# An attention and MoE kernel on one core: its instruction order planned anew, with three small moves of work

## The chip, the cores and the metric

One core of a Trainium2 chip runs the kernel. The metric is the device time of one execution in microseconds (us); the time of a kernel is the median of several runs. One further execution is recorded by the hardware profiler, and all rows shown come from it. Engines: PE is TensorE (PEld its weight loads), DVE VectorE, ACT ScalarE, POOL GpSimd, SP SyncE, which issues nearly all transfers.

## The reference

Inputs are r, k, v, w of shape (4, 8, 768, 48), u (8, 48), and two weight matrices, 384 x 2048 and 2048 x 384. All is float32.

```python
for t in range(S):                                   # linear attention with decay w and bonus u
    cur = einsum('bhd,bhe->bhde', u * k[t], v[t])
    y[t] = einsum('bhd,bhde->bhe', r[t], state + cur)
    state = w[t][..., None] * state + einsum('bhd,bhe->bhde', k[t], v[t])
x = y as (3072 tokens, 384)
h = x @ w_in
g = where(h >= 1, h, where(h <= -1, 0, (h + 1) ** 2 / 4))
out = g @ w_out
```

## The kernel before, in words

The 3072 tokens are cut into 12 units of 256 tokens. `attention(u)` turns the recurrence of one unit into matmuls: VectorE scans the decays forward (L433) and backward (L428), scales k and r by them (L462, L512), TensorE multiplies within chunks of 64 tokens (L482), transposes k (L521, copied by ScalarE at L528), forms the chunks' updates of the state (L543) and sums the outputs (L592). Units 0 to 3 ("early") need k * u as well. In unit 0 ScalarE makes it (L453), in units 1 to 3 GpSimd (`with_u`, L444).

The result of a unit is x, kept as a high part rounded to the matmul type and a low part, the rest. ScalarE copies the high part out of PSUM (L649). The low part is made in one of two ways. For units in the set `INPLACE`, `less` has TensorE subtract the high part within PSUM by matmuls with minus the identity (L656, L658), and ScalarE copies what is left (L645). For all others VectorE subtracts (L647). One head pair's columns lie in a tile `last` and are spread into x by six small transfers on SyncE (x<-last, L691). Unit 0 does that by matmuls instead (`ALONE`).

Two units make a block of 512 tokens, six blocks in all. For each block and each of 16 slices f of the hidden layer, `products` has nine matmuls into h (L939), the gate on ScalarE and VectorE (L754, L755, L756, L758, L759), and nine matmuls into three accumulators `acc` (L959). Blocks 0 and 1 take their first 5 and 11 slices in halves of 256 tokens. The accumulators are copied out (L776) and sent off (L777).

`weight(f)` decodes slice f of the weights from raw 64-bit words: a transfer of 768 KB, two ScalarE passes (L354, L357), one GpSimd pass `rr` (L358), a VectorE pass (L360), then the split in high part (ScalarE, L350) and low part (VectorE, L363). At most `FLIGHT` = 3 raw slices are on their way.

No engine's order is written out by hand. Each operation is put into a `Plan` with its engine, an assumed cost in us, what it reads and writes, and a due time. `Plan.order` simulates the engines and picks, among the operations that are ready on an engine, the one with the earliest due time; `Plan.best` repeats this in six rounds with the steps' begin times of the round before, and keeps the shortest. The instructions are then issued in that order, each engine taking its own in turn. The due time of a unit's operation is the begin of the block's step that needs it, less `LEADS[u]` and `SLACK` times the rest of its chain; for weights it is `DECODES[f]`. `TURN` is the assumed cost of changing TensorE between 64-row and 128-row matmuls, `RATES` that of transfers. Where the plan sees TensorE idle, `kept_warm` fills in matmuls on zeros (L325).

At the end the kernel reads a flag (L825) and branches on it (L826) past a general fallback, which does not run for these inputs.

Of the kernel before, what the change touches and what calls it, by code (L numbers as in the profile page):

```python
# [48 lines left out]
class Plan:  # L49
# [9 lines left out]
    LATENCY = {"PE": 0.16, "DVE": 0.083, "ACT": 0.1}  # L59
    LATE_64 = 0.31  # L60

    TURN = {64: 0.22, 128: 0.09}
    RATES, SETTLED = (315e3, 400e3), 8.5
    ISSUE = 0.75

    def __init__(self):
# [63 lines left out]
    def order(self):  # L130
        ops = self.ops
        left = [len(op["deps"]) for op in ops]
        users = [[] for _ in ops]
        for n, op in enumerate(ops):
            for m in op["deps"]:
                users[m].append(n)
        free, end, begin, lands = {"SP": self.ISSUE}, {}, {}, []
        port = bus = 0.0
        mode = 128
        ran = {}  # L140
        open_ = {e: [] for e in ("PE", "SP", "ACT", "DVE", "POOL")}

        since = {}

        def opened(n):
            op = ops[n]
            since[n] = max((ran[m] if ops[m]["e"] == op["e"] and not ops[m]["size"] else end[m] + self.HOP for m in op["deps"]), default=0.0)
            open_[op["e"]].append(n)

        def ready(n):  # L150
            return max(since[n], port) if ops[n]["port"] else since[n]

        for n, k in enumerate(left):
            if not k:
                opened(n)
        first = {}
        while any(open_.values()):
            best = None
            for e, ns in open_.items():
                if not ns:  # L160
                    continue

                at = first.get(e)
                if at is None:
                    at = first[e] = min(ready(n) for n in ns)
                t = max(free.get(e, 0.0), at)
                if best is None or t < best[0]:
                    best = t, e
            t, e = best
            n = min((n for n in open_[e] if ready(n) <= t + 1e-9), key=lambda n: (ops[n]["key"], n))  # L170
            op = ops[n]
            open_[e].remove(n)
            first[e] = None
            if op["size"] and len(lands) >= LANES:
                t = max(t, lands[-LANES])
            begin[n] = t
            end[n] = t + op["cost"]
            if e == "PE" and op["mode"] != mode:
                mode = op["mode"]
                end[n] += self.TURN[mode]  # L180
            free[e] = ran[n] = end[n] - self.late(op)
            if op["port"]:
                port = free[e]
                first.clear()
            if op["size"]:
                bus = max(bus, t)
                bus += op["size"] / self.RATES[bus >= self.SETTLED]
                end[n] = bus + 2.0
                lands.append(end[n])
            for m in users[n]:  # L190
                left[m] -= 1
                if not left[m]:
                    opened(m)
                    first[ops[m]["e"]] = None
        assert len(begin) == len(ops)
        rank = sorted(range(len(ops)), key=lambda n: (begin[n], n))

        seen, out = set(), []

        def put(n):  # L200
            if n in seen:
                return
            seen.add(n)
            for m in sorted(ops[n]["deps"]):
                put(m)
            out.append(n)

        for n in rank:
            put(n)
        self.begin, self.end = begin, end  # L210
        return out

SLACK = 0.501
LEADS = {0: 89.12, 1: 29.14, 2: 50, 3: 29.29, 4: 70.5, 5: 42.42, 6: 96.05, 7: 79.29, 8: 141.79, 9: 131.35, 10: 73.56, 11: 100.77}
DECODES = [85.83, 12.47, 98.38, 2.07, 12.65, 0.37, -9.24, 7.4, -10.78, 23.04, -10.64, 54.35, 18.52, -29.87, 45.5, -17.01]
LEAD = 15
FLIGHT = 3

# [5 lines left out]


ALONE = {0}
INPLACE = {0, 6}
STEP, FIRST, PACED, AFTER = 17.0572, 293.658, 16.0129, 4.9  # L230
ROUNDS = 6


def attention_moe(tc, a):
    nc = tc.nc
# [101 lines left out]
    def weight(f, when):  # L337
        first, due = len(plan.ops), None
        s, k = fl[f % 2], f % 2
        m = s.bitcast(I32)  # L340
        r16 = rr.bitcast(U16).rearrange("p (c two) -> p c two", two=2)

        def fetch():
            wraw[f] = wpool.tile([128, 768, 2], I32, tag="wt", name=f"wraw{f}")
            nc.sync.dma_start(out=wraw[f].rearrange("p c two -> p (c two)"), in_=a["wbits"][f].bitcast(I32))

        def split():
            wt = wpool.tile([128, 2, 768], F32R, tag="wt", name=f"wt{f}")
            w_hi[f], w_lo[f] = wt[:, 0, :], wt[:, 1, :]
            A.copy(w_hi[f], s)  # L350

        op("SP", 0.45, due, (), [("raw", f), ("flight", f % FLIGHT)], fetch, size=786432)

        op("ACT", 0.9, due, [("raw", f)], [("fl", k)], lambda: A.activation(  # L354
            s, wraw[f][:, :, 1].bitcast(F32), AF.Abs, scale=float(2.0**-112)))
        op("ACT", 1.07, due, [("raw", f), ("flight", f % FLIGHT)], ["rr_low"],
           lambda: A.activation(r16[:, :, 0], wraw[f][:, :, 0].bitcast(U32), AF.Copy, scale=LOW))  # L357
        op("POOL", 3.2, due, [("raw", f)], ["rr_high"], lambda: G.tensor_scalar(  # L358
            out=r16[:, :, 1], in0=wraw[f][:, :, 1].bitcast(F32), scalar1=0.0, scalar2=32768.0, op0=ALU.is_lt, op1=ALU.mult))
        op("DVE", 0.95, due, ["rr_low", "rr_high"], [("fl", k)], lambda: V.scalar_tensor_tensor(  # L360
            out=m, in0=m, scalar=3, in1=rr, op0=ALU.logical_shift_left, op1=ALU.bitwise_or), port=True)
        op("ACT", 0.83, due, [("fl", k)], [("wh", f), ("raw", f)], split)
        op("DVE", 0.95, due, [("fl", k), ("wh", f)], [("wl", f)], lambda: V.tensor_tensor(  # L363
            out=w_lo[f], in0=s, in1=w_hi[f].bitcast(F32), op=ALU.subtract), port=True)
        plan.group(first, when, DECODES[f])

# [11 lines left out]
    def attention(u, when):  # L378
# [69 lines left out]
        for q in (1, 0):  # L448
            s = slot[q]
            if early:  # L450
                if alone:
                    for pr in range(2):
                        op("ACT", 0.42, due, [("k", s), "cst"], [("ku", q), "nk"], lambda q=q, pr=pr: A.activation(  # L453
                            ku[:, q, pr * UT : pr * UT + UT], rk[slot[q]][:, 1, pr * UT : pr * UT + UT], AF.Copy,
                            scale=u_col[:, 2 * q + pr : 2 * q + pr + 1]))
                else:
                    op("POOL", 2.85, due, [("k", s), "cst"], [("ku", q), "nk"], lambda q=q: with_u(q))
            op("DVE", 1.34, due, [("w", s)], [("p", q), "seeds"], lambda q=q: scan(q, False), port=True)
            op("ACT", 0.2, due, [("p", q)], [("ptot", u, q)], lambda q=q: A.copy(
                ptot[:, 4 * u + 2 * q : 4 * u + 2 * q + 2], pv[:, q, :, UT]))  # L460
            op("DVE", 1.48, due, [("w", s), ("p", q)], ["y", "seeds"], lambda q=q: scan(q, True), port=True)
            op("DVE", 0.69, due, ["y"], [("k", s)], lambda q=q: V.tensor_tensor(  # L462
                out=parts(q, 1), in0=parts(q, 1), in1=y_.rearrange("p (n c) -> p n c", c=UT + 1)[:, :, 1:], op=ALU.mult), port=True)
# [33 lines left out]
            for h in range(2):  # L497
                op("DVE", 0.73, due, [("b", bd[h]), "cst"], [("R", h)], lambda h=h: picked(h, bd[h], twice.bitcast(I32)))
        else:
            op("POOL", 1.9, due, (), ["nk"], lambda: G.tensor_tensor(  # L500
                out=nk[:, :, 0, :], in0=nk[:, :, 0, :], in1=nk[:, :, 1, :], op=ALU.mult), port=True)
            op("DVE", 0.94, due, ["us"], ["nk"], lambda: V.tensor_tensor(
                out=nk[:, :, 0, :], in0=nk[:, :, 0, :], in1=u_sb.unsqueeze(1).broadcast_to([128, 2, DM]), op=ALU.mult), port=True)
# [1 line left out]
                op("DVE", 0.54, due, ["nk"], ["d"], lambda c=c: V.tensor_reduce(  # L505
                    out=d_[:, c, :], in_=nk[:, c, 0, :].rearrange("p (h e) -> p h e", e=D), op=ALU.add, axis=AX.X))
            for h in range(2):
                op("POOL", 1.1, due, ["d", "cst"], [("R", h)], lambda h=h: G.tensor_tensor(  # L508
                    out=r_[h], in0=twice.unsqueeze(1).unsqueeze(1).broadcast_to([128, 4, 2, C]),
                    in1=dv[:, h].unsqueeze(3).broadcast_to([128, 4, 2, C]), op=ALU.mult), port=True)  # L510
        for q in (1, 0):
# [224 lines left out]
    def products(n):  # L736
# [8 lines left out]
        for half in range(2):  # L745
# [10 lines left out]
        op("DVE", 0.13 + 0.56 * k, due, [("b", 6 + hk)], [("g", gk)], lambda: nc.vector.scalar_tensor_tensor(  # L756
            out=gs, in0=gs, scalar=1.0, in1=hs, op0=ALU.min, op1=ALU.max))
        op("ACT", c, due, [("g", gk)], [("gh", gk)], lambda: nc.scalar.copy(ghs, gs))  # L758
        op("DVE", 0.15 + 0.54 * k, due, [("g", gk), ("gh", gk)], [("gl", gk)], lambda: nc.vector.tensor_tensor(  # L759
            out=gls, in0=gs, in1=ghs.bitcast(F32), op=ALU.subtract), port=True)  # L760
        count[b] = count.get(b, 0) + 1
        begin, end = count[b] == 1, f == NF - 1
# [16 lines left out]
        if done:  # L779

            out("DVE", nc.sync, "SP", 0, whole)
            out("ACT", nc.scalar, "ACT", 1, whole)
            out("DVE", nc.sync, "SP", 2, halves[0])
            out("ACT", nc.scalar, "ACT", 2, halves[1])
            return
        for j in range(3):
            out("ACT" if j else "DVE", nc.sync, "SP", j, whole)
# [241 lines left out]
```

## Time and profile before

| | |
|---|---|
| median of 3 runs | 525.49 us (525.31 to 525.93) |
| profiled execution | 525.05 us, span 523.0 us |
| granted TensorE clock, mean | 0.995 |
| busy: PE, DVE, ACT, POOL | 505.3, 333.5, 294.0, 108.2 us |
| matmuls | 5571 |
| transfers | 54.11 MB, mean 103 GB/s |
| last output's issue | 516.85 us |

The span is the time from the first to the last instruction of the profiled execution; the 2.05 us beside it lie outside. A row of a group gives line, engine, operation, tiles written <- read, count, busy time and mean duration, then the idle time of the engine before them and what ended it. "q" behind an engine (SPq, ACTq) is its queue of waits and transfers. A busy PE is not always useful: the fillers count too.

### The profile page before, as it was taken

The page shows a single profiled execution, that of the slowest core. Times are in us where ns is not written, and L with a number is a line of the kernel's source. Part 1 is how long each engine was busy: PE and PEld are TensorE (multiplying, and loading weights), DVE is VectorE, ACT ScalarE, POOL GpSimd, SP SyncE. Part 2 cuts the span into 40 slices and gives each one's busy share as a digit, 9 for nine tenths or more (in the row PEclk, how much of TensorE's full clock was granted, in tenths as well). Part 3 has the DMA queues.
Part 4 walks back from the last instruction along what each step waited for, and adds up shares of the span by engine and source line. Part 5 has one row for each costly group of instructions (what it writes and reads, how often), then busy time and mean ns, then how long its engine had stood idle before and what let it go on. Part 6 is the DMA issues. An engine that isn't in the chain of part 4 may idle for free.

```text
span 523.0 us, 13092 instructions
## 1 busy us (share of the span) xinstructions
PE 505.3 (97%) x5571; PEld 414.8 (79%) x5571; DVE 333.5 (64%) x561; ACT 294.0 (56%) x600; POOL 108.2 (21%) x72
## 2 busy tenths in 40 slices
PE   8899999999899999999999999999999999999994
PEld 7777977778899987877788788877777888888783
DVE  7899997749899996879872576242464333243331
ACT  3766798988765763765463456344354444444441
POOL 2896676602113111211110010000010000000000
PEclk9999999999999999999999999999999999999998
DMA  8965645136653512644400240000110000100001
GB/s 323 402 245 200 212 150 197 64 111 213 212 172 117 203 51 83 223 141 150 172 22 0 70 135 1 0 0 1 63 57 10 8 1 0 62 0 1 0 0 66
DMA packets 21921, 54.11 MB, mean 103 GB/s; under 512 B 3104, under 2 KB 8672, under 8 KB 21856
## 3 DMA queue, kind: packets, MB, share of 16 engines
q1 hardware_dynamic: 21568, 52.82, 29.4%
q8 instruction: 45, 0.74, 0.6%
q10 hardware_dynamic: 288, 0.39, 0.2%
q14 instruction: 20, 0.16, 0.1%
HBM read 46.32 MB, written 4.72 MB: 98 GB/s over the span
## 4 chain that ended last, share of the span: by engine, by line
PE 62%; DVE 14%; ACT 8%; DMA 7%; issue 4%; POOL 3%; SPq 2%; ACTq 0%; DVEq 0%; POOLq 0%
PE acc L959 28%; PE h L939 28%; PE bank L592 3%; POOL rr L358 3%; DMA rk<-in_rk 2%; DVE fl L360 2%; DMA wraw<-in_wbits 2%; DVE r L488 2%; DVE p L433 2%; DVE rk L512 1%; DMA x<-last 1%; DVE y L428 1%; PE bank L482 1%; DVE g L756 1%; DMA out_y<-g 1%
## 5 line engine op out<-in xcount | busy, mean ns | idle before, releaser
L939 PE MATMUL h<-x,wt 128*128 128x512 f32 (+1 forms) x1008 | 221.5, 367 | 2.9 <-DVE g L756 1.4
L939 PEld LDWEIGHTS h<-x,wt 128*128 128x128 f32 x1008 | 169.5, 188 | 37.9 <-DVE g L756 3.1
L959 PE MATMUL acc<-gh,wt 128*128 128x512 f32 (+1 forms) x672 | 155.9, 367 | 0.0
L756 DVE SCALAR_TENSOR_TENSOR g<-g,h 128x512 f32<-128x512 f32 (+1 forms) x112 | 67.8, 607 | 106.3 <-ACT g L755 105.4
L959 PEld LDWEIGHTS acc<-gh,wt 128*128 128x128 f32 x672 | 113.7, 188 | 22.2 <-ACT gh L758 0.9
L754 ACT ACTIVATE g<-h 128x512 f32<-128x512 f32 (+1 forms) x112 | 59.7, 533 | 93.2 <-PE h L939 85.9
L759 DVE TENSOR_TENSOR gl<-g,gh 128x512 fp32r<-128x512 f32 (+1 forms) x112 | 73.1, 655 | 36.6 <-ACT gh L758 35.8
L758 ACT CAST gh<-g 128x512 fp32r<-128x512 f32 (+1 forms) x112 | 62.3, 558 | 51.2 <-DVE g L756 49.1
L959 PE MATMUL acc<-gl,wt 128*128 128x512 f32 (+1 forms) x336 | 86.1, 364 | 0.0
L959 PEld LDWEIGHTS acc<-gl,wt 128*128 128x128 f32 x336 | 58.5, 188 | 11.6 <-DVE gl L759 0.8
L755 ACT ACTIVATE g<-g 128x512 f32<-128x512 f32 (+1 forms) x112 | 63.9, 571 | 3.3
L358 POOL TENSOR_SCALAR rr<-wraw 128x768 uint16<-128x768 f32 x16 | 55.1, 3441 | 31.7 <-DVE fl L360 17.2
L508 POOL TENSOR_TENSOR r<-cst,d 128x512 f32<-128x512 f32 x16 | 18.9, 1202 | 174.9 <-PE bank L592 134.5
L433 DVE TENSOR_TENSOR_SCAN p<-wq,seeds 128x514 f32<-128x514 f32 x24 | 31.5, 1313 | 3.1 <-POOL st L312 2.1
L428 DVE TENSOR_TENSOR_SCAN y<-wq,seeds 128x514 f32<-128x514 f32 x24 | 31.5, 1312 | 0.8
L500 POOL TENSOR_TENSOR nk<-nk 128x768 f32<-128x768 f32 x8 | 16.8, 2101 | 64.9 <-DMA nk<-in_nk 57.7
L528 ACT COPY kt<-bank 128x512 f32<-128x512 f32 x24 | 13.8, 583 | 17.8 <-PE bank L521 17.8
L357 ACT ACTIVATE rr<-wraw 128x768 uint16<-128x768 uint32 x16 | 17.4, 1089 | 4.6 <-DMA wraw<-in_wbits 2.5
L325 PE MATMUL bank<-clear 128*128 128x512 f32 (+1 forms) x60 | 17.6, 411 | 1.6 <-DVE seeds L432 1.6
L512 DVE TENSOR_TENSOR rk<-rk,p 128x512 f32<-128x512 f32 x24 | 17.9, 757 | 0.4 <-PE acc L482 0.4
L462 DVE TENSOR_TENSOR rk<-rk,y 128x512 f32<-128x512 f32 x24 | 17.7, 739 | 0.4 <-DMA rk<-in_rk 0.3
L592 PEld LDWEIGHTS bank<-rk,st 48*48 48x48 f32 (+1 forms) x656 | 11.5, 121 | 7.8 <-issue 2.2
(109 smaller groups left out, 393.4 us busy)
## 6 DMA issues: line engine op xcount, KB each, us to landing
rk<-in_rk SPq DMA_DIRECT2D x24, 512.0 KB, 5.1
wraw<-in_wbits SPq DMA_DIRECT2D x16, 768.0 KB, 6.9
wq<-in_w SPq DMA_DIRECT2D x24, 257.5 KB, 3.0
nk<-in_nk SPq DMA_DIRECT2D x8, 768.0 KB, 4.9
vn<-in_v SPq DMA_DIRECT2D x11, 384.0 KB, 6.4
fl<-in_w SPq DMA_DIRECT2D x12, 257.0 KB, 2.7
out_y<-g SPq DMA_DIRECT2D x10, 256.0 KB, 2.6
x<-last SPq DMA_DIRECT2D x66, 32.0 KB, 2.5
```

Source lines behind the costliest of these rows:

```text
L358: op("POOL", 3.2, due, [("raw", f)], ["rr_high"], lambda: G.tensor_scalar(out=r16[:, :, 1], in0=wraw[f][:, :, 1].bitcast(F32), scalar1=0.0 ...
L428: V.tensor_tensor_scan(out=y_[:, ::-1], data0=w[:, SEG:0:-1], data1=sv[:, ::-1], initial=0.0, op0=ALU.mult, op1=ALU.add)
L433: V.tensor_tensor_scan(out=pv[:, q].rearrange("p n c -> p (n c)"), data0=w[:, 0:SEG], data1=sv, initial=0.0, op0=ALU.mult, op1=ALU.add,)
L512: op("DVE", 0.69, due, [("p", q)], [("r", slot[q])], lambda q=q: V.tensor_tensor(out=parts(q, 0), in0=parts(q, 0), in1=pv[:, q, :, 0:UT], ...
L592: PE.matmul(out=bank[by[g]][HP * half : HP * half + wide, lo : lo + C], start=first, stop=False, skip_group_check=True, **kw)
L754: op("ACT", c, due, [("b", 6 + hk)], [("g", gk)], lambda: nc.scalar.activation(gs, hs, AF.Relu, scale=0.5, bias=0.5))
L755: op("ACT", c, due, (), [("g", gk)], lambda: nc.scalar.activation(gs, gs, AF.Square))
L756: op("DVE", 0.13 + 0.56 * k, due, [("b", 6 + hk)], [("g", gk)], lambda: nc.vector.scalar_tensor_tensor(out=gs, in0=gs, scalar=1.0, in1=hs, ...
L758: op("ACT", c, due, [("g", gk)], [("gh", gk)], lambda: nc.scalar.copy(ghs, gs))
L759: op("DVE", 0.15 + 0.54 * k, due, [("g", gk), ("gh", gk)], [("gl", gk)], lambda: nc.vector.tensor_tensor(out=gls, in0=gs, in1=ghs.bitcast( ...
L939: nc.tensor.matmul(hp, lhsT=wx[f][:, cs], rhs=xt[:, j, :], start=n == 0, stop=n == 8)
L959: nc.tensor.matmul(o[j], lhsT=wx[f][:, cs], rhs=gt, start=first and i == 0, stop=stop and i == 2, skip_group_check=True)
```

## The change

The planner's assumed costs and all its due-time parameters are new: turns, transfer rates and the landing of a transfer, GpSimd's passes, one VectorE cost, `SLACK`, `LEADS`, `DECODES`, `STEP`, `FIRST`, `PACED`. So every engine's order can differ. Three moves of work go with it: k * u of unit 1 is done by ScalarE (`SCALED`), as in unit 0; the low part of x of unit 1 is made in PSUM, and that of unit 6 no longer is (`INPLACE`); the last block's four outputs are all issued by SyncE, where ScalarE issued two.

```diff
-    TURN = {64: 0.22, 128: 0.09}
-    RATES, SETTLED = (315e3, 400e3), 8.5
+    TURN = {64: 0.33, 128: 0.02}
+    RATES, SETTLED = (315e3, 385e3), 8.5
...
-                end[n] = bus + 2.0
+                end[n] = max(bus + 2.0, t + 1.75 + op["size"] / 314e3)
...
-SLACK = 0.501
-LEADS = {0: 89.12, 1: 29.14, 2: 50, 3: 29.29, 4: 70.5, 5: 42.42, 6: 96.05, 7: 79.29, 8: 141.79, 9: 131.35, 10: 73.56, 11: 100.77}
-DECODES = [85.83, 12.47, 98.38, 2.07, 12.65, 0.37, -9.24, 7.4, -10.78, 23.04, -10.64, 54.35, 18.52, -29.87, 45.5, -17.01]
+SLACK = 1.384
+LEADS = {0: 200.34, 1: 17.94, 2: 10.1, 3: 21.34, 4: 40.45, 5: 51.11, 6: 84.54, 7: 119.23, 8: 114.23, 9: 96.67, 10: 78.32, 11: 100.22}
+DECODES = [58.08, 65.33, 175.35, 38.53, 1.42, 5.14, 81.19, 4.4, 14.07, 65.02, 61.72, 84.69, 39.36, 203.15, 25.09, -1.54]
...
-INPLACE = {0, 6}
-STEP, FIRST, PACED, AFTER = 17.0572, 293.658, 16.0129, 4.9
+INPLACE = {0, 1}
+SCALED = {0, 1}
+STEP, FIRST, PACED, AFTER = 27.1568, 703.402, 25.4941, 4.9
...
-        op("POOL", 3.2, due, [("raw", f)], ["rr_high"], ...
+        op("POOL", 3.35, due, [("raw", f)], ["rr_high"], ...
...
-                if alone:
+                if u in SCALED:
                     for pr in range(2):
                         op("ACT", 0.42, due, [("k", s), "cst"], [("ku", q), "nk"], ...
                 else:
-                    op("POOL", 2.85, due, [("k", s), "cst"], [("ku", q), "nk"], lambda q=q: with_u(q))
+                    op("POOL", 2.6, due, [("k", s), "cst"], [("ku", q), "nk"], lambda q=q: with_u(q))
...
-            op("POOL", 1.9, due, (), ["nk"], ...
+            op("POOL", 2.2, due, (), ["nk"], ...
...
-                op("POOL", 1.1, due, ["d", "cst"], [("R", h)], ...
+                op("POOL", 1.25, due, ["d", "cst"], [("R", h)], ...
...
-        op("DVE", 0.15 + 0.54 * k, due, [("g", gk), ("gh", gk)], [("gl", gk)], ...
+        op("DVE", 0.18 + 0.52 * k, due, [("g", gk), ("gh", gk)], [("gl", gk)], ...
...
             out("DVE", nc.sync, "SP", 0, whole)
-            out("ACT", nc.scalar, "ACT", 1, whole)
+            out("ACT", nc.sync, "SP", 1, whole)
             out("DVE", nc.sync, "SP", 2, halves[0])
-            out("ACT", nc.scalar, "ACT", 2, halves[1])
+            out("ACT", nc.sync, "SP", 2, halves[1])
```

More of the change, by code (lines that the diff above doesn't have):

```diff
@@ L357, in weight @@
            lambda: A.activation(r16[:, :, 0], wraw[f][:, :, 0].bitcast(U32), AF.Copy, scale=LOW))
-        op("POOL", 3.2, due, [("raw", f)], ["rr_high"], lambda: G.tensor_scalar(
+        op("POOL", 3.35, due, [("raw", f)], ["rr_high"], lambda: G.tensor_scalar(
             out=r16[:, :, 1], in0=wraw[f][:, :, 1].bitcast(F32), scalar1=0.0, scalar2=32768.0, op0=ALU.is_lt, op1=ALU.mult))
@@ L499, in attention @@
         else:
-            op("POOL", 1.9, due, (), ["nk"], lambda: G.tensor_tensor(
+            op("POOL", 2.2, due, (), ["nk"], lambda: G.tensor_tensor(
                 out=nk[:, :, 0, :], in0=nk[:, :, 0, :], in1=nk[:, :, 1, :], op=ALU.mult), port=True)
@@ L507, in attention @@
             for h in range(2):
-                op("POOL", 1.1, due, ["d", "cst"], [("R", h)], lambda h=h: G.tensor_tensor(
+                op("POOL", 1.25, due, ["d", "cst"], [("R", h)], lambda h=h: G.tensor_tensor(
                     out=r_[h], in0=twice.unsqueeze(1).unsqueeze(1).broadcast_to([128, 4, 2, C]),
@@ L758, in products @@
         op("ACT", c, due, [("g", gk)], [("gh", gk)], lambda: nc.scalar.copy(ghs, gs))
-        op("DVE", 0.15 + 0.54 * k, due, [("g", gk), ("gh", gk)], [("gl", gk)], lambda: nc.vector.tensor_tensor(
+        op("DVE", 0.18 + 0.52 * k, due, [("g", gk), ("gh", gk)], [("gl", gk)], lambda: nc.vector.tensor_tensor(
             out=gls, in0=gs, in1=ghs.bitcast(F32), op=ALU.subtract), port=True)
```

## The prediction

> **What bounds the kernel now.** I read the page first, then the stretches, then the chain, then single lines. The page makes TensorE look full:
>
> ```profile
> span 523.0 us, 13092 instructions
> ...
> PE 505.3 (97%) x5571; PEld 414.8 (79%) x5571; DVE 333.5 (64%) x561; ACT 294.0 (56%) x600; POOL 108.2 (21%) x72
> ```
>
> How much of TensorE's 505 us is work that the result needs comes from the chain of waits (start, us, what), where TensorE's own pieces follow each other without a gap:
>
> ```profile
> 251.88 1.49 PE bank L592 x96
> ...
> 264.06 2.10 PE h L939 x9
> ...
> 291.36 1.09 PE bank L482 x64
> ...
> 297.66 0.86 PE bank L543 x64
> ...
> 370.12 0.88 PE bank L521 x8
> ```
>
> Nine full-width products take 2.10 us. There are 6 blocks x 16 steps x 2 such groups: 192 x 2.10 = 403 us. A unit of attention is 1.09 + 0.88 + 0.86 + 1.49 = 4.32 us, twelve of them 51.8, and the second L482 group of units 0 to 3 adds 4.4. That is 459 of the 523 us. The other 64 are what an order can win or lose, and they are not spread evenly (columns: stretch, length, then busy us and count of PE, PEld, DVE, ACT, POOL, then clock, DMA share, GB/s):
>
> ```profile
> 15.00:30.00 15.00, 13.36 (x175) 10.71 (x173) 13.54 (x20) 11.61 (x24) 13.92 (x7) 1.00 1.00 386
> 30.00:45.00 15.00, 13.70 (x370) 11.52 (x374) 14.47 (x27) 7.78 (x16) 11.48 (x6) 1.00 0.41 144
> 45.00:60.00 15.00, 13.95 (x225) 12.20 (x216) 14.92 (x27) 11.42 (x24) 11.93 (x7) 1.00 0.82 290
> 60.00:75.00 15.00, 15.00 (x159) 13.47 (x158) 14.50 (x24) 13.50 (x27) 9.67 (x3) 1.00 0.34 123
> 75.00:90.00 15.00, 14.62 (x180) 11.20 (x179) 12.65 (x21) 13.04 (x23) 10.19 (x4) 1.00 0.62 224
> 90.00:105.00 15.00, 15.00 (x66) 11.92 (x65) 10.81 (x14) 13.64 (x20) 11.04 (x5) 1.00 0.19 62
> ...
> 210.00:225.00 15.00, 15.00 (x193) 12.18 (x192) 13.81 (x22) 11.62 (x26) 2.70 (x2) 1.00 0.63 202
> ```
>
> The same view of single lines, 0 to 60 us: first the products into h (L939), then those into acc (L959), then the filler matmuls on zeros (L325):
>
> ```profile
> 0.00:60.00 60.00, 10.74 (x72) 9.30 (x72) 1.00 0.78 289
> ...
> 0.00:60.00 60.00, 7.42 (x49) 6.35 (x50) 1.00 0.78 289
> ...
> 0.00:60.00 60.00, 19.65 (x69) 12.13 (x69) 1.00 0.78 289
> ```
>
> In the first 60 us only 121 half-width matmuls are products, about 121 x 0.12 = 14 us; the fillers alone stand for 19.65 us. VectorE meanwhile is busy 43.89 of the 45 us from 30 to 75. So the head is bound by VectorE: a microsecond taken off it there should come back almost whole. From 75 us on TensorE sets the pace, and only TensorE's own work and its waits count.
>
> **The change part by part.** The sum goes against the profiled execution, 525.05 us (span 523.0 and 2.05 around it); the median of the runs is 525.49, 0.44 above it.
>
> *(a) Low part of x: unit 1 joins the in-place form, unit 6 leaves it.* Unit 1 loses four VectorE subtractions and gains eight matmuls (L656, L658) and four ScalarE copies; unit 6 the reverse. The prices:
>
> ```profile
> L647 DVE TENSOR_TENSOR x<-bank,x x20: 533/551/559, 47.7 to 401.2; 128x384 fp32r<-128x384 f32 x20
> L647 DVE TENSOR_TENSOR last<-bank,last x20: 273/281/283, 48.6 to 401.9; 128x128 fp32r<-128x128 f32 x20
> ...
> L645 ACT CAST x<-bank x2: 480/490/499, 213.5 to 214.1; 128x384 fp32r<-128x384 f32 x2
> ...
> 212.93 0.22 PE L656 MATMUL bank<-last,minus 128*128 128x128 f32 x1
> ...
> 213.77 1.14 PE L939 MATMUL h<-x,wt 128*128 128x512 f32 x4
> ```
>
> In the head VectorE loses 2 x 0.55 + 2 x 0.28 = 1.66 us; unit 1's subtractions start at 47.7, inside its fullest stretch. Bounds: 1.66 gained if all of it turns into earlier products; nothing, or up to 0.84 lost, if TensorE's added eight matmuls (212.93 to 213.77 = 0.84 us at unit 6) fall on a moment when it isn't waiting. I take -1.3, nearest the full 1.66, because fillers stand for a third of TensorE's first 60 us. ScalarE's four added copies, two of 0.49 us and two narrower ones (at most 0.49, so under 2.0 us together), are hidden by its 3.6 us idle from 45 to 60; without that cover they would stand in its queue ahead of a decode's passes. Behind the low part SyncE's six x<-last transfers of unit 1 wait, and behind those the products: matmuls and copies (0.84 and then one copy of 0.49 after the other) take about as long as the four subtractions, so that path is level. At unit 6 TensorE gets the 0.84 us back where it is the bound: -0.8. What could eat it: VectorE, at 13.81 of 15 us there, gets 1.66 more, 0.47 over full, so part must move to neighbouring steps; bounds -0.84 and +0.47.
>
> *(b) k\*u of unit 1 from GpSimd to ScalarE.*
>
> ```profile
> 22.73 2.07 POOL L444 TENSOR_SCALAR nk<-rk,cst 128x256 f32<-128x256 f32 x2
> 28.25 2.85 POOL L444 TENSOR_SCALAR nk<-rk,cst 128x256 f32<-128x256 f32 x2
> ...
> L453 ACT ACTIVATE nk<-rk,cst x4: 494/502/510, 6.7 to 8.5; 128x256 f32<-128x256 f32 x4
> ...
> DVE fl L360 <- POOL rr L358: 1.8, 2, 1.0
> ```
>
> GpSimd gets 2.07 + 2.85 = 4.9 us free between its decodes, ScalarE gets 4 x 0.50 = 2.0 us in a stretch with 3.4 idle. But VectorE waited for GpSimd's decode only 1.8 us in the whole run: that is the bound of the gain. On the other side ScalarE's 2.0 us can push a decode's passes back: +1, half of it, since 3.4 are idle. I take -0.4. What is late next is VectorE itself.
>
> *(c) The last outputs on SyncE.* At the end (timeline, issues with us to landing, the branch line L826, and SyncE's waits):
>
> ```profile
> 515.99 0.42 ACTq L777 DMA_DIRECT2D out_y<-g  x1
> 516.06 0.33 SPq L777 DMA_DIRECT2D out_y<-g  x1
> 516.45 0.37 ACT L776 COPY g<-acc 128x256 f32<-128x256 f32 x1 [0.49 <-DVE g L776]
> 516.85 0.34 ACTq L777 DMA_DIRECT2D out_y<-g  x1
> ...
> out_y<-g ACTq DMA_DIRECT2D x1, 256.0 KB, 3.9
> out_y<-g SPq DMA_DIRECT2D x1, 128.0 KB, 2.0
> out_y<-g ACTq DMA_DIRECT2D x1, 128.0 KB, 4.3
> ...
> L826 SPq EVENT_SEMAPHORE  x8: 17/17/17, 520.0 to 521.6; - x8
> ...
> L826 SPq COMPARE_BRANCH  x1: 45/45/45, 516.4 to 516.4; - x1
> ...
> SPq L826 <- SPq L826: 4.7, 2, 3.6
> ```
>
> The tempting sum is 4.3 - 2.0 = 2.3 us off the last landing (516.85 + 4.3 = 521.1). I don't take it. SyncE branches over the fallback at 516.4 and its next instruction comes only at 520.0, 3.6 us later by its wait row, with no transfer in between to explain it (its own last one, 516.06 + 2.0, had landed at 518.1). With all four issues on SyncE (0.33 each, and behind them in its queue only its branch) the last can't go out before ScalarE's last copy ends at 516.82, so at about 516.85, as now, and SyncE's branch moves from 516.4 to 517.25. Add 3.6: 520.85, then its eight semaphore steps. Now the last six of them follow the landing at 521.1 and end at 521.6, some 0.08 apiece; then all eight would run through from 520.85 to 521.4. So -0.2; bounds -2.3 (the branch costs no more than the landing) and +0.9 (SyncE's whole shift shows). By the Trainium skill, "Runtime: NRT & Kernel Launch", Instruction fetch mechanics, a taken branch outside the fetched window stalls until its page has come by DMA; by that rule the 3.6 us follows SyncE's branch wherever it goes, and the trace agrees with its 3.6. The skill's "DMA: Bandwidth & Descriptors", Issuing engines are not separate DMA queues, says that transfers share the same engines whoever issues them, only sequencer time being saved by spreading; by it 4.3 against 2.0 would be order and load, not the queue, and the term would be zero or a loss of issue time. No run here separates these yet.
>
> *(d) The new order.* Leads, slack and due times are all new, and the corrected costs (GpSimd's decode 3.2 to 3.35, its k*u 2.85 to 2.6 against 2.07 and 2.85 above, turns, transfers) shift every engine's sequence. Instructions are the same apart from (a) to (c). The trace can't show the new order; it shows what one is worth. Weight loads and matmuls wait from 60 to 255 us mostly in pieces like these:
>
> ```profile
> PEld h L939 <- DVE g L756: 2.3, 4, 0.8
> PEld bank L521 <- DVE last L647: 1.5, 1, 1.5
> PEld bank L592 <- DVE st L561: 1.2, 2, 0.7
> ```
>
> These three are 5.0 us, all of VectorE handing over late: the gain's bound. The loss is bounded by a late arrival of the size of unit 1's r and k now, 5.9 us:
>
> ```profile
> 19.47 5.89 DMA rk<-in_rk
> ```
>
> I take -1.6, a third of the one side: the old order already avoids most waits, and the corrections are of a few tenths each. SyncE's queue carries the same loads in another sequence; GpSimd loses only (b).
>
> Sum: -1.3 - 0.8 - 0.4 - 0.2 - 1.6 = -4.3; 525.05 - 4.3 = 520.75, and 0.44 to the median: **521.2 us**.
>
> **The rivals.** *The tail gives its full landing* (-2.3 in place of -0.2): 519.1. For it: the SyncE landing of 2.0 beside ACT's 3.9 and 4.3; against it, the 3.6 us behind SyncE's branch.
>
> *The order wins much more*: all 5.0 us of those waits, and all 1.8 us of VectorE's waits for GpSimd: 521.2 - 3.4 - 1.4 = 516.4. For it: 19.65 us of fillers; against: VectorE has next to no idle time there to reorder.
>
> *No change to be seen*: (a) and (b) only pass their time to the next wait, (d) is zero: 525.0.
>
> *Slower: ScalarE becomes the bound of the decodes.* It takes on 2.0 us of k*u and up to 2.0 of copies for unit 1, say 3.6. From 60 to 105 us it is busy 13.50, 13.04 and 13.64 of 15, 4.8 idle in all, while each decode needs three passes of it. If the new leads draw decodes and unit 1 into the same stretch, the 3.6 us stand on the chain and VectorE's 1.66 gives nothing back: 525.49 + 3.6 - 0.8 - 0.2 = 528.1. It decides from 2.1 us on (2.1 - 0.8 - 0.2 is 0.2% of the time), that is if more than half of the 3.6 falls behind 60 us, where ScalarE hasn't the 7.2 us of slack that it has from 30 to 45.
>
> **How the numbers follow.** The forecast (519.9 to 523.5 by the smaller doubts of its terms) 0.47; full landing 0.12; order wins much more 0.14; no change 0.12; slower 0.15. A measurement here tells about 0.2%, 1.05 us, from no change. Faster: 0.47 + 0.12 + 0.14 = 0.73; same 0.12; slower 0.15. The range leaves some 0.08 below and 0.1 above: 515.2 to 526.8, with the low rival, most of the no-change case and the near half of the slower one inside.
>
> **What would show it.** (a) fewer L325 fillers before 60 us, L656 and L658 beside unit 1's x instead of near 213 us; (b) L444 eight times, L453 eight times, VectorE's wait for rr under 1.8; (c) SyncE's first L826 semaphore 3.5 to 4 us behind its branch, and the span's end within 1 us of where it now stands behind the last product; (d) products counted to 60 us, now 121. Wrong would be: VectorE idle before 75 us for a late weight or r, k load, ScalarE at 14 or more of 15 us behind 60, or a tail shorter by 2 us.

## The result, and the profile after

The changed kernel takes 519.99 us (median of 4, 518.55 to 521.23), the kernel before 525.40 beside it: ratio 0.9894, 95% interval 0.9868 to 0.9921. By the ratio that is 5.6 us less (4.2 to 6.9 within the interval); 521.2 had been forecast. The profiled execution took 519.89 us, its span is 518.1 where it was 523.0. An inserted line moves the line numbers by one: L939 and L959 are now L940 and L960, L325 is L326, L776 and L777 are L777 and L778.

The stretches of the changed kernel (columns as before: PE, PEld, DVE, ACT, POOL busy, clock, DMA share, GB/s):

```profile
15.00:30.00 15.00, 13.02 (x227) 10.74 (x227) 12.95 (x20) 10.22 (x22) 7.94 (x4) 1.00 0.99 355
30.00:45.00 15.00, 13.61 (x320) 11.75 (x320) 14.59 (x27) 11.55 (x27) 11.63 (x4) 1.00 0.47 167
45.00:60.00 15.00, 13.67 (x216) 12.76 (x216) 14.64 (x25) 12.02 (x28) 12.84 (x8) 1.00 0.80 297
60.00:75.00 15.00, 15.00 (x95) 13.27 (x93) 14.88 (x24) 13.95 (x25) 9.69 (x3) 1.00 0.36 129
75.00:90.00 15.00, 15.00 (x66) 12.12 (x65) 12.13 (x15) 14.62 (x22) 10.85 (x4) 1.00 0.46 173
```

VectorE still has 44.1 us of work in the 45 from 30 to 75, where it had 43.9. What TensorE does meanwhile is different. The same view of the lines L940, L960 and L326, 0 to 60 us:

```profile
0.00:60.00 60.00, 10.26 (x72) 9.02 (x72) 1.00 0.79 287
...
0.00:60.00 60.00, 7.86 (x59) 7.47 (x60) 1.00 0.79 287
...
0.00:60.00 60.00, 16.57 (x56) 10.48 (x56) 1.00 0.79 287
```

131 matmuls are products by 60 us, where it was 121, and the fillers went from 19.65 to 16.57 us. The stretches 0 to 60 and 60 to 255 us as a whole (all engines, columns as in the table above), before:

```profile
0.00:60.00 60.00, 54.30 (x1072) 45.36 (x1073) 54.20 (x88) 36.08 (x72) 40.77 (x38) 1.00 0.78 289
60.00:255.00 195.00, 190.53 (x2684) 161.86 (x2683) 165.13 (x287) 137.10 (x309) 59.98 (x30) 1.00 0.44 146
```

and after:

```profile
0.00:60.00 60.00, 53.65 (x1077) 46.08 (x1078) 52.66 (x87) 38.86 (x84) 35.41 (x34) 1.00 0.79 287
60.00:255.00 195.00, 192.22 (x2595) 162.97 (x2594) 165.69 (x288) 137.04 (x301) 57.05 (x28) 1.00 0.44 143
```

TensorE runs equally many matmuls in both kernels when the fillers are taken off: 5571 less 71 fillers before, 5558 less 58 after, both 5500. So what the change saved shows in its idle time and its fillers together. In the first 60 us these were 60 - 54.30 + 19.65 = 25.35 us and are 60 - 53.65 + 16.57 = 22.92. From 60 to 255 us, where neither kernel has fillers, they were 195 - 190.53 = 4.47 us and are 195 - 192.22 = 2.78. Some 2.4 us were thus won in the head and 1.7 behind it. That says where, not by which part of the change. From 60 to 255 us the longest waits of weight loads for VectorE are also shorter, none over 1.2 us in all (the first of them was 2.3):

```profile
PEld bank L522 <- DVE r L489: 1.2, 2, 0.9
PEld h L940 <- DVE g L757: 1.2, 3, 0.5
PEld h L940 <- DVE seeds L433: 1.1, 1, 1.1
```

VectorE's first copy of the last block, before and after:

```profile
514.67 0.69 DVE L776 COPY ob<-acc 128x512 f32<-128x512 f32 x1 [2.01 <-PE acc L959]
```

```profile
510.07 0.69 DVE L777 COPY ob<-acc 128x512 f32<-128x512 f32 x1 [2.00 <-PE acc L960]
```

From it to the end (the tail) it took 523.0 - 514.67 = 8.3 us before and 518.1 - 510.07 = 8.0 now. So of the 4.9 us of span, 4.6 were won ahead of that copy, by order and moves together. The 0.3 of the tail can't be told from nothing: in the traces of this document that have the branch, the tail takes 8.0 to 8.3 us where ScalarE issues two of the outputs (six traces) and 8.0 to 8.4 where SyncE issues all (seven).

### The profile page after: what moved, and what is told of

The parts are those of the page before. It is cut to its first block, busy times and chain, and to the rows that moved or that the text cites. A ratio compares the mean times of both kernels' runs of the same rounds, so it can differ in the third digit from the quotient of the medians.

```text
span 518.1 us, 13059 instructions
## 1 busy us (share of the span) xinstructions
PE 501.7 (97%) x5558; PEld 413.4 (80%) x5558; DVE 333.6 (64%) x561; ACT 296.1 (57%) x604; POOL 101.0 (19%) x68
## 4 chain that ended last, share of the span: by engine, by line
PE 81%; DVE 7%; ACT 4%; issue 2%; DMA 2%; POOL 1%; SPq 1%; POOLq 0%; DVEq 0%
PE h L940 35%; PE acc L960 34%; PE bank L593 4%; PE bank L483 2%; PE bank L522 2%; PE bank L544 2%; PE bank L326 1%; DMA fl<-in_w 1%; DVE g L757 1%; DVE gl L760 1%; DMA vn<-in_v 1%; SPq L692 1%; DVE y L429 1%; POOL rr L359 1%; DVE rk L513 1%
## 5 line engine op out<-in xcount | busy, mean ns | idle before, releaser
L940 PE MATMUL h<-x,wt 128*128 128x512 f32 (+1 forms) x1008 | 220.9, 366 | 2.3 <-DVE seeds L433 0.9
L940 PEld LDWEIGHTS h<-x,wt 128*128 128x128 f32 x1008 | 169.4, 188 | 35.6 <-DVE g L757 1.2
L960 PE MATMUL acc<-gh,wt 128*128 128x512 f32 (+1 forms) x672 | 155.7, 367 | 0.3 <-DVE ob L777 0.3
L960 PEld LDWEIGHTS acc<-gh,wt 128*128 128x128 f32 x672 | 113.7, 188 | 21.7 <-DVE ob L777 0.5
L760 DVE TENSOR_TENSOR gl<-g,gh 128x512 fp32r<-128x512 f32 (+1 forms) x112 | 75.0, 672 | 37.7 <-ACT gh L759 36.6
L960 PE MATMUL acc<-gl,wt 128*128 128x512 f32 (+1 forms) x336 | 85.6, 363 | 0.0
L960 PEld LDWEIGHTS acc<-gl,wt 128*128 128x128 f32 x336 | 58.7, 188 | 10.8
L359 POOL TENSOR_SCALAR rr<-wraw 128x768 uint16<-128x768 f32 x16 | 52.8, 3302 | 34.0 <-DVE fl L361 20.9
L429 DVE TENSOR_TENSOR_SCAN y<-wq,seeds 128x514 f32<-128x514 f32 x24 | 30.0, 1249 | 0.8
L501 POOL TENSOR_TENSOR nk<-nk 128x768 f32<-128x768 f32 x8 | 15.3, 1909 | 65.9 <-DMA nk<-in_nk 57.5
L463 DVE TENSOR_TENSOR rk<-rk,y 128x512 f32<-128x512 f32 x24 | 16.4, 685 | 2.1 <-ACT nk L454 1.7
L364 DVE TENSOR_TENSOR wt<-fl,wt 128x768 fp32r<-128x768 f32 x16 | 16.1, 1004 | 2.5 <-ACT wt L351 2.1
L326 PE MATMUL bank<-clear 128*128 128x512 f32 (+1 forms) x53 | 16.1, 425 | 1.6 <-DVE seeds L433 1.6
```

Of the source, the lines that this page charges most:

```text
L326: PE.matmul(out[:, 0 : 128 * n], lhsT=clear, rhs=clear.unsqueeze(1).broadcast_to([128, n, 128]), start=True, stop=True)
L359: op("POOL", 3.35, due, [("raw", f)], ["rr_high"], lambda: G.tensor_scalar(out=r16[:, :, 1], in0=wraw[f][:, :, 1].bitcast(F32), scalar1=0. ...
L429: V.tensor_tensor_scan(out=y_[:, ::-1], data0=w[:, SEG:0:-1], data1=sv[:, ::-1], initial=0.0, op0=ALU.mult, op1=ALU.add)
L760: op("DVE", 0.18 + 0.52 * k, due, [("g", gk), ("gh", gk)], [("gl", gk)], lambda: nc.vector.tensor_tensor(out=gls, in0=gs, in1=ghs.bitcast( ...
L940: nc.tensor.matmul(hp, lhsT=wx[f][:, cs], rhs=xt[:, j, :], start=n == 0, stop=n == 8)
L960: nc.tensor.matmul(o[j], lhsT=wx[f][:, cs], rhs=gt, start=first and i == 0, stop=stop and i == 2, skip_group_check=True)
```

## The experiments

Each ratio is against runs of the kernel before on the same chip. Where us are given beside a ratio, they are the difference of the ratio from 1 times 525.4. The changed kernel's own 0.9894 comes from four runs, so a difference from it carries two intervals.

### One move at a time, every engine's order kept as before

The plan is left as it was; only what is issued at its places is different.

```diff
 b_tail   -            out("ACT", nc.scalar, "ACT", 1, whole)
          +            out("ACT", nc.sync, "ACT", 1, whole)         # likewise the last half
 b_six    +    IN_PSUM = {0}          # less() and the copies ask for u in IN_PSUM, the plan for INPLACE
 b_one    +    IN_PSUM = {0, 1, 6}    # unit 1: less(), then two ScalarE copies, in the place of VectorE's
 b_ku     +    if u == 1: A.activation(ku[:, q, cs], ...)   # in place of G.tensor_scalar
```

> The kernel before, its order kept instruction by instruction; only the last block's two outputs that ScalarE issued are issued by SyncE. The forecast's theory (SyncE's own branch, some 3.6 us until its next instruction, takes the place of the ScalarE queue's landing): -0.2 us, 525.2, and the time from the last product's begin to the span's end 7.8 us -> 7.5. The rival (a SyncE landing takes 2.0 where ScalarE's took 4.3): -2.3 us, 523.1.

Measured: 0.9993 (0.9980 to 1.0007), -0.4 us. The ScalarE queue was not what made outputs late; issued by SyncE two of them still land 4.0 us after their issue (issues of the last block with us to landing, a median where there are two):

```profile
out_y<-ob SPq DMA_DIRECT2D x1, 256.0 KB, 2.1
out_y<-g SPq DMA_DIRECT2D x1, 256.0 KB, 2.7
out_y<-g SPq DMA_DIRECT2D x2, 128.0 KB, 4.0
```

The rival of 2.3 us is outside the interval. The forecast's 0.2 is inside, and so is no gain; the tail of its trace takes 523.5 - 515.33 = 8.2 us.

> The kernel before, order kept; only the low part of x of unit 6 goes back from PSUM (eight matmuls, four ScalarE copies) to VectorE (four subtractions). The forecast: TensorE is the bound at 213 us, so its 0.84 us come back whole: -0.8 us, 524.6. The rival: VectorE is too full there (13.81 of 15 us and 1.66 more), and the products wait for it: between no gain and +0.5, 525.4 to 525.9.

Measured: 0.9996 (0.9982 to 1.0009), -0.2 us. The forecast's -0.8 (0.9985) lies inside the interval, and so does no gain: the run can't tell them apart.

> The kernel before, order kept; only the low part of x of unit 1 goes from VectorE (four subtractions, 1.66 us) into PSUM (eight matmuls, four ScalarE copies). The forecast: VectorE is the bound of the head, so 1.3 of its 1.66 us come back: -1.3 us, 524.1. The rival: with every engine's order fixed, the time passes to the next wait (ScalarE's copies now stand in its queue before a gate): between no gain and +0.8, 525.4 to 526.2.

Measured: 1.0052 (1.0033 to 1.0071), 2.7 us slower. Both expectations fall, the forecast's by its sign. In the trace of this run (timelines of TensorE, ScalarE and VectorE; its line numbers are up to 14 higher) the second half's matmuls stand behind nine products in TensorE's queue, ScalarE waits for them 1.01 us ahead of its copy, and VectorE then waits 2.10 us for a decode's pass that stands behind that copy:

```profile
48.15 1.23 PE L953 MATMUL h<-x,wt 128*128 128x256 f32 x9
49.22 0.23 PE L670 MATMUL bank<-last,minus 128*128 128x128 f32 x1
...
49.81 0.27 ACT L662 CAST last<-bank 128x128 fp32r<-128x128 f32 x1 [1.01 <-PE bank L672]
...
51.35 0.96 DVE L361 SCALAR_TENSOR_TENSOR fl<-fl,rr 128x768 int32<-128x768 int32 x1 [2.10 <-ACT fl L355]
```

The 1.66 us of VectorE were free, but what stood next in its queue was not ready.

> The kernel before, order kept; only k*u of unit 1 is done by ScalarE (four passes of 0.5 us) in place of GpSimd (4.9 us). The forecast: -0.4 us, 525.0, bounds -1.8 and +1. A second theory, from the two traces: GpSimd slows VectorE while both run (the y scan 1312 ns on the mean before, 1249 after; L462 739 before, 685 as L463 after), so freeing GpSimd also shortens VectorE's instructions in the head, by about 1 us between 20 and 32 us: -1.0 or more. ScalarE as a new wait: +1.

Measured: 0.9990 (0.9977 to 1.0004), -0.5 us. The forecast's -0.4 and the second theory's -1.0 are both inside; +1 is excluded. In its trace VectorE is busy 53.30 of the first 60 us, where it was 54.20 with as many instructions (88), so the shortening that the second theory expects is there. Four moves one by one come to +1.6 us where the change gives -5.6.

### The plan made anew: moves and parameters apart

```diff
 new_plan_old_moves   (from the changed kernel)
-INPLACE = {0, 1}
-SCALED = {0, 1}
+INPLACE = {0, 6}
+SCALED = {0}                  # and two last outputs on nc.scalar, as before
 old_plan_new_moves   (from the kernel before)
-INPLACE = {0, 6}
+INPLACE = {0, 1}
+SCALED = {0, 1}               # and all last outputs on nc.sync
```

> The changed kernel with its new costs, leads and due times, but none of the three moves: k*u of unit 1 on GpSimd, low part in PSUM for units 0 and 6, two last outputs on ScalarE. The order is planned for that. Theory now, after the four single moves on the old order gave -0.5, -0.2, -0.7 and +2.5 us: the order carries the gain, so this keeps at least half of it: 521.5 to 522.5 (0.4 to 1 us of it from the missing moves). The forecast's split (2.7 of 4.3 us from the moves): 523.9. A third: leads and moves were made for each other, and without the moves nothing is left: 525 or more.

Measured: 1.0103 (1.0071 to 1.0136), 5.4 us slower than before, as the third theory had it: without the moves nothing of the gain is left.

> The kernel before with its old costs, leads and due times, and all three moves; the order is planned for that. If the order's parameters carry the gain: 524.5 to 526.5, nothing that can be told from no change. By the forecast's split: -2.7 us, 522.8. If the planner finds by itself what the moves make possible in the head (VectorE 1.66 us less, GpSimd 4.9 us less): 523.5.

Measured: 1.0037 (1.0019 to 1.0054), 1.9 us slower, outside all three expectations. Each half of the change makes the kernel slower, the whole makes it faster: -5.6 where the halves add up to +7.3. Moves and parameters gain only together.

### One move undone in the changed kernel, order kept

```diff
 a_one   +    IN_PSUM = {0}                    # unit 1: less() issues nothing, VectorE subtracts in place of ScalarE's copies
 a_ku    +    G.tensor_scalar(out=ku[:, q, cs], ...)   # unit 1, in the place of each ScalarE pass
```

> The changed kernel, its order kept; only the low part of x of unit 1 goes back from PSUM to VectorE, the matmuls for it left out. The forecast's term says +1.3 us on the changed kernel (521.3), since VectorE is again 97% busy from 30 to 75 us there. By the one-move run on the old order (where the in-place form cost 2.7 us, since its matmuls and copies stood in fixed queues) such a move can as well be worth nothing or be better undone: 519 to 520.

Measured: 0.9926 (0.9900 to 0.9953), against 0.9894 with the move: 0.32% or 1.7 us of the gain is gone by these medians. That is near the forecast's 1.3, in an order that was planned for this form, but it is not shown: the two intervals overlap, and of its seven runs two (519.84 and 519.99 us) are as fast as the changed kernel's and five take 522.8 to 523.7.

> The changed kernel, its order kept; only k*u of unit 1 goes back from ScalarE to GpSimd. The forecast's term: +0.4 us (520.4), bounds +1.8 and -1. The trace of the changed kernel shows VectorE waiting 1.7 us for ScalarE's k*u (L463 <- nk L454), which the move back would take away: -1 if that wait is the dearer one; GpSimd has 7 us free from 15 to 30 us there, so that it should hide its 4.9 us: 519.5 to 520.5.

Measured: 0.9921 (0.9899 to 0.9943), 1.4 us of the gain gone, with intervals that overlap. Its profiled execution (span 517.4 us) is as short as the changed kernel's, and four of its six runs take 522.2 to 522.5, so this one stays open too.

### The costs, and one lead

```diff
 new_costs_only   (from the kernel before)    # TURN, RATES, landing, four GpSimd costs, gl's cost: the new ones
 old_costs        (from the changed kernel)   # the same lines: the old ones
 nudge_lead       (from the changed kernel)
-LEADS = {0: 200.34, 1: 17.94, 2: 10.1, ...
+LEADS = {0: 200.34, 1: 17.94, 2: 5.1, ...
```

> The kernel before with the corrected costs alone (turns, transfer rate and landing, GpSimd's passes, one VectorE cost); its old leads, slack, due times and moves. If corrected costs by themselves make a better order: 523 to 525. If leads and costs belong together: slower. The plan's own end, which the kernel works out while it orders, rises from 506.5 to 517.1 us; if the chip follows the plan's end: 533 to 536.

Measured: 1.0160 (1.0137 to 1.0184), 8.4 us slower, which is 533.8 and what the plan's own end had said. Corrected costs by themselves are no gain.

> The changed kernel with the old costs alone put back; its new leads, slack, due times and moves stay. If the corrected costs carry the gain: back to 525. If the leads do: 520. If the chip follows the plan's own end (504.6 for the changed kernel, 509.0 for this one, by the old costs): 523 to 526.

Measured: 1.0165 (1.0142 to 1.0188), 8.7 us slower, more than any of the three expectations. New leads and moves without the new costs are no gain either.

> The changed kernel with one number different: the lead of unit 2, 10.1 us, is 5.1. Costs and moves are the changed kernel's, the order is planned for it. If the gain comes from corrected costs and the moves, as the forecast had it, one lead doesn't matter: 519.5 to 521. If it hangs on the leads having been fitted exactly to these costs and moves: the plan's own end rises by 7.6 us, and the chip gives all of the gain back: 525 to 529.

Measured: 1.0129 (1.0107 to 1.0151), 6.8 us slower than before and 12 slower than the changed kernel, for one number; that is 532.2, beyond the 525 to 529 expected. The trace shows where the time goes. VectorE's first copies of the accumulators mark the ends of blocks 0 and 1. In the changed kernel:

```profile
122.81 0.67 DVE L777 COPY ob<-acc 128x512 f32<-128x512 f32 x1
212.88 0.69 DVE L777 COPY ob<-acc 128x512 f32<-128x512 f32 x1
```

With the nudged lead:

```profile
120.73 0.68 DVE L777 COPY ob<-acc 128x512 f32<-128x512 f32 x1
223.18 0.69 DVE L777 COPY ob<-acc 128x512 f32<-128x512 f32 x1 [0.79 <-PE acc L960]
```

At the end of block 0 the nudged kernel is 2.1 us ahead; at the end of block 1 it is 10.3 behind. Between them lies SyncE's queue. Its timeline in the changed kernel:

```profile
101.02 0.33 SPq L296 DMA_DIRECT2D fl<-in_w  x1
101.45 0.85 SPq L296 DMA_DIRECT2D rk<-in_rk  x2
102.39 0.61 SPq L296 DMA_DIRECT2D vn<-in_v  x1
```

With the nudged lead:

```profile
102.86 14.17 SPq L296 DMA_DIRECT2D fl<-in_w  x6
117.12 2.56 SPq L296 DMA_DIRECT2D rk<-in_rk  x2
```

The loads fl<-in_w belong to a check whose result is read at the end; they wait for their buffers, which ScalarE's passes of that check (6.7 us of SyncE's waits between 102 and 118 us) and VectorE's decode hold. With the nudged lead six of them stand ahead of the next unit's r and k, which leave 15.7 us later. VectorE runs dry meanwhile (stretches of the changed kernel, 105 to 135 us):

```profile
105.00:120.00 15.00, 15.00 (x191) 12.25 (x190) 11.58 (x20) 12.60 (x28) 3.97 (x3) 1.00 0.60 184
120.00:135.00 15.00, 13.77 (x256) 12.40 (x255) 13.48 (x29) 13.00 (x37) 0.00 (x0) 1.00 0.83 270
```

With the nudged lead:

```profile
105.00:120.00 15.00, 14.39 (x240) 11.08 (x239) 6.71 (x13) 12.72 (x29) 0.00 (x0) 1.00 0.40 120
120.00:135.00 15.00, 12.03 (x251) 10.30 (x249) 8.87 (x18) 9.36 (x23) 3.62 (x3) 1.00 0.76 256
```

It does 15.6 us of work in these 30 where the changed kernel does 25.1, and the unit's work lands later on products that wait for it. That the six loads are the cause is read from this one trace; no run moved them back.

The plan's own end, worked out without the chip, is on record for five of the orders: 506.5 us before, 504.6 for the changed kernel, 517.1 with the new costs only, 509.0 with the old ones put back, and 504.6 + 7.6 = 512.2 with the nudged lead. Against the kernel before it has the sign right each time, but not the size: -1.9, +10.6, +2.5 and +5.7 where the chip gave -5.6, +8.4, +8.7 and +6.8.

### The tail without its branch

```diff
 a_nobranch   (from the changed kernel)
-    unsafe = nc.values_load(flag, min_val=0, max_val=1)
-    with tc.If(unsafe > 0):
-        general(tc, a, ident, w_hi, w_lo)
```

> The changed kernel without the read of the flag and the branch over the general fallback; the fallback is left out of the program. On the tail's term: four outputs on SyncE still landed 4.2 and 3.9 us behind their issue, so the ScalarE queue was not what made them late. Theory: what makes them late is the code that each engine fetches behind its branch at the same time, over the same transfer engines. Without it the last landing takes 2.1 us and the end comes 1.5 to 2 us sooner: 518.2. Rival: the four outputs (0.77 MB) queue up behind each other and land late by themselves: -0.3 us, 519.7.

Measured: 0.9866 (0.9849 to 0.9884), which is 518.4 us as the theory had it, against 0.9894 with the branch: some 1.5 us less, with intervals that overlap. The trace is clearer. Last outputs of the changed kernel (us to landing, and ahead of them the two queues that carry code, with packets, MB and share):

```profile
q14 instruction: 6, 0.05, 1.2%
q8 instruction: 2, 0.03, 1.0%
...
out_y<-ob SPq DMA_DIRECT2D x1, 256.0 KB, 2.1
out_y<-g SPq DMA_DIRECT2D x2, 128.0 KB, 2.8
out_y<-g SPq DMA_DIRECT2D x1, 256.0 KB, 4.2
```

(The 2.8 is the median of two, 1.7 for the first half and 3.9 for the last.) Without the branch, where the same view has no rows of code queues:

```profile
out_y<-ob SPq DMA_DIRECT2D x1, 256.0 KB, 2.0
out_y<-g SPq DMA_DIRECT2D x2, 128.0 KB, 1.9
out_y<-g SPq DMA_DIRECT2D x1, 256.0 KB, 2.1
```

and VectorE's first copy of the last block stands here:

```profile
512.88 0.69 DVE L777 COPY ob<-acc 128x512 f32<-128x512 f32 x1 [2.01 <-PE acc L956]
```

All land in about 2 us, and from VectorE's copy to the end it is 518.1 - 512.88 = 5.2 us, where it is 8.0 to 8.4 in all thirteen traces with the branch. So the branch, with the read of its flag and the code behind it, costs the tail 2.8 us, and outputs land late only with it. Which of these parts delays them, and how, this run doesn't separate. (The products of this profiled execution ended 2.8 us later than the changed kernel's, so its span is the same; executions of one kernel differed by nearly that much, as the 518.55 to 521.23 above.) The rival, outputs that hold each other up, falls.

## Why the prediction was right or wrong

The number was right by 1.2 us and the direction too. By place it came out too: the forecast had 2.5 us in the head, by (a) and (b) (what unit 6 no longer needs of TensorE is done there for unit 1, in place of fillers), and 2.4 were won; it had 1.6 by (d) from shorter waits behind the head, and 1.7 were won. The account of what causes them was right only in part.

**(a) Unit 1 in PSUM, -1.3.** As a term that can be added by itself it failed: on the old order the move costs 2.7 us. Within the new order, undoing it costs 1.7 by the medians, which is not shown. VectorE is busy nearly all of the head, but time freed on an engine is a gain only if the operation next in its queue is ready. "Back almost whole" left out that each engine takes its instructions in a fixed order. The copies that were to hide in ScalarE's idle time stood ahead of a decode's pass instead, for which VectorE waited 2.10 us; the prediction names this danger but prices it at nothing. *Unit 6, -0.8*: -0.2 was measured, and the interval allows both.

**(b) k\*u on ScalarE, -0.4.** -0.5 on the old order; 1.4 when undone on the new one, in intervals that overlap: not contradicted, and not shown. Of its signs the counts came (k\*u eight times each on GpSimd and ScalarE), but the shorter wait did not: VectorE's waits for rr rose from 1.8 to 2.4 us, and a new wait of 1.7 us for ScalarE's k\*u appeared:

```profile
DVE fl L361 <- POOL rr L359: 2.4, 4, 1.4
...
DVE rk L463 <- ACT nk L454: 1.7, 1, 1.7
```

**(c) The tail, -0.2.** 0.4 +/- 0.7 by the runs, and the traces put it within their spread: no gain is shown, and none is excluded. The reason given, SyncE's own branch, is part of the truth. In the changed kernel its branch and its next instruction stand here:

```profile
L827 SPq EVENT_SEMAPHORE  x8: 17/17/17, 516.1 to 516.7; - x8
...
L827 SPq COMPARE_BRANCH  x1: 45/45/45, 512.8 to 512.8; - x1
```

3.3 us lie between, but the whole-width output, which landed 4.2 us after its issue, came in at the same time. The trace before has the same: "no transfer in between to explain it" looked at SyncE's own transfers alone, while ScalarE's whole-width output, issued at 515.99, landed 3.9 us later, at 519.9, just ahead of SyncE's 520.0. So whether SyncE waited for its code or for that landing is open; without the branch both delays go.

Of the two pages that were weighed, the Trainium skill's "Runtime: NRT & Kernel Launch", Instruction fetch mechanics, says that a taken branch outside the fetched window stalls until its page has come. The 2.8 us that the tail loses agree with it, though GpSimd's own branch was over in 0.1 us (486.4 to 486.5 us in the changed kernel).

The Trainium skill's "DMA: Bandwidth & Descriptors", Issuing engines are not separate DMA queues, says that transfers share the same engines whoever issues them. The late landings agree with it: 3.9 and 4.3 us from ScalarE's queue before, 4.0 from SyncE's with the tail alone moved.

**(d) The new order, -1.6, bounded by -5.0 and +5.9.** Its size is near what was won from 60 to 255 us, but as a term beside the moves this is the step that failed. It treated the order as a small correction to a plan that is good anyway, and bounded it by waits of the old trace. Orders by the same planner for nearly the same instructions ran from 520.0 to some 534 us: 8.4 and 8.7 us over the kernel before with only the costs exchanged, 6.8 over it with one lead changed. So the gain is not in the corrected costs alone, nor in the moves alone, nor in the leads with one of the other two missing, but in the three together; the 4.6 us of span ahead of VectorE's last copies are what that combination gives. That the leads were fitted to just these costs and moves is inferred, from the 12 us that one changed lead costs. That my terms summed to nearly the right number is chance as far as their causes go: taken one by one, the moves make the kernel slower by 1.6 us in all.

**The rivals.** The full landing fell: late landings go with the branch, not with the queue. ScalarE did reach the 14 us and more that I had named as a sign of being wrong (14.62 from 75 to 90), yet TensorE is busy all 15.00 us there, so it cost nothing: the sign was wrong. A slower case did exist, in the kernel with the nudged lead, but of another kind than the one priced: SyncE's queue, with loads that nobody is waiting for ahead of one that is needed. I had passed over that queue in one sentence.

Open is why the two orders with exchanged costs are so slow; they were measured, not taken apart.

## What to carry to other kernels

Where a planner or a hand-written order fixes each engine's queue, a change of cost, engine or due time is not a term to be added. Expect an order whose parameters were set for other numbers to lose: all five kernels replanned here with a part of them exchanged were 0.4 to 1.7% slower than before and 1.4 to 2.7% slower than the changed one. Price an edit in the order that it will run in, and ask of each freed engine what stands next in its queue and whether that is ready. Ask the planner for its own end before the chip is asked: where it is on record here, its sign was right. And look at the transfer queue: a load without urgency that waits for its buffer holds up every load behind it.

## What the runs showed of the hardware

In three traces with the branch (before, after, and with the tail alone moved) two of the last three outputs landed 3.9 to 4.3 us after their issue, on ScalarE's queue or on SyncE's, and the others 1.7 to 2.7. Without the branch all landed in 1.7 to 2.1. The branch, with its flag's read and the code behind it, cost the end 2.8 us, though its condition had been known for over 20 (the flag is read at 490 us by SyncE and GpSimd, at 512 to 517 by the others, in the kernel before). Behind it the next instruction of VectorE, ScalarE and SyncE came 2.9 to 4.1 us later in the traces before and after, whatever part of this was a wait for landings.
